# Feature-map attention and a cosine feed-forward on one core: the second products of a kept value in two steps, under a new order table

## The chip, the cores and the metric

One core of a Trainium2 chip runs the program. The metric is device time in microseconds (us). The engines are named as in the profile: PE (TensorE), DVE (VectorE), ACT (ScalarE), POOL (GpSimd) and SP (SyncE, which issues the DMAs here); PEld is PE's weight load.

## The reference

```python
def phi(x):                                    # x: batch 8, heads 8, 576 positions, 64
    proj = np.einsum('bhsd,df->bhsf', x, w_phi)             # 128 features
    proj = proj - np.max(np.abs(proj), axis=-1, keepdims=True)
    return np.concatenate([np.exp(proj), np.exp(-proj)], axis=-1)
q_p, k_p = phi(q), phi(k)
kv = np.einsum('bhsf,bhsd->bhfd', k_p, v);  z = np.sum(k_p, axis=2)
num = np.einsum('bhsf,bhfd->bhsd', q_p, kv)
den = np.einsum('bhsf,bhf->bhs', q_p, z)[..., None] + 1e-06
x = (num / den) as 4608 tokens x 512
h = x @ w_in                                   # 512 x 2048
out = (h * np.cos(h)) @ w_out                  # 2048 x 512, float32
```

## The kernel before

**The work.** Attention runs in 32 units of two heads each. A unit loads its q and k (`qk`, L530), projects q (L548, L551) and k (L594, L619), takes maxima, exponentiates on ACT, multiplies k's features with v (L698, L704) and q's features with that (L733, L739), divides on DVE, turns the result and stores it to DRAM (L770, L774). The first units have two `qk` tiles to take turns in; from the 22nd on all use one.

The feed-forward works on columns of 512 tokens. A float32 product is made of three matmuls: each operand is split into a high part (ACT, helper line L50) and a low part (DVE, helper line L55), and high·high, high·low and low·high are added up in a PSUM bank. Three columns go through `visit` (nine visits, L860 the first product, L907 to L909 the second). Six columns go in three pairs through `visit_two`, which makes the products of 2 x 2 blocks with seven multiplications instead of eight. Its first half (`products`, L1090) makes h; `wave` makes h·cos(h) with ACT and DVE (L1196, L1199, L1202, L1209) and keeps the values in tiles that other work has left. Its second half, `sweep`, goes over the kept values seven times: it combines some of them (DVE, L1257), splits each into `gh` (ACT) and `gl` (DVE) and multiplies them with slices of w_out that SP loads from DRAM (L1247) into the rings `wo_h` and `wo_l`, two tiles each.

**The second product before.** For one kept value, `mm2` in `sweep` (L1293) issues six matmuls as one step, three into each of two banks: `gh` with the slice's high part, `gh` with its low part, `gl` with its high part. The step depends on DVE's low step. `mm2` in `visit` does the same with four banks, two of them in a step (L907 gh, L908 gh, L909 gl). `gh` and `gl` are rings of three tiles.

**What sets the order.** All of this is written as `Step` objects with an engine and dependencies. `ORDER`, a table of step numbers written out by hand, says in which order the steps are issued; each engine executes its own steps in that order and waits in order. The costs in `Step` and its flag `port` (an operation of DVE or POOL that works on SBUF alone) enter no instruction; `plan` takes the order from the table and PSUM banks from who is last free. ACT loads another function table (`ACT_TABLE_LOAD`, L1435) wherever the order goes from a step with the sine to one with the exponential or back. Nothing but the order of issue and the semaphores of real dependencies keeps DVE and POOL apart.

Of the kernel before, what the change touches and what calls it, by code (L numbers as in the profile page):

```python
# [17 lines left out]
P = 128  # L18
# [8 lines left out]
def phi_attention_then_cos_ffn(ctx: ExitStack, tc: tile.TileContext, qkT, vS, w_phi, w_in, w_out, out, outT):  # L27
# [42 lines left out]
    class Step:  # L70
        def __init__(self, eng, cost, fn, deps=(), take=(), use=(), lat=None, table=None, port=False, kind="", pipe=0.0):
# [10 lines left out]
            for b in self.take + self.use:  # L82
# [5 lines left out]
    SHAPE = dict(mm1="full", mm2="full", one="full", wide="full", k_mm="upper", k_end="full", q_end="full", k_sub="full", kv_mm="left", x_mm="left", q_mm="upper")  # L88
    ORDER = [0, 3, 5, 4, 7, 8, 6, 9, 42, 58, 10, 11, 1, 44, 59, 46, 18, 60, 1265, 45, 64, 23, 61, 65, 66, 12, 48, 62, 17, 63, 19, 21, 13, 1266, 47, 24, 20, 68, 22,
# [701 lines left out]
    held = {}  # L791
# [3 lines left out]
    def visit(v):  # L795
# [46 lines left out]

        acc = [Buf("bank") for _ in range(NB3)]
        done = {}
        before = None
        for i, pr in enumerate(pairs):
            first, last = i == 0, i == len(pairs) - 1
            m = {}
# [29 lines left out]
            for r in range(2):  # L878
# [42 lines left out]
                for tbs in [[tb] for tb in range(NB3)] if fine else [[0, 1], [2, 3]]:  # L921
# [3 lines left out]
                    for tb in tbs:  # L925
                        done[tb] = before
                if first:
                    begun = before
# [573 lines left out]
```

## Time and profile before

| | |
|---|---|
| median of 3 runs | 993.64 us (993.25 to 995.34) |
| the profiled execution | 992.14 us |
| its span, first to last instruction | 990.4 us |
| PE, DVE, ACT, POOL busy | 99%, 86%, 80%, 21% of the span |
| granted TensorE clock | full in all slices |
| bytes moved | 211.67 MB, 214 GB/s |

Busy time of PE is the union of its matmuls' records. A record of a matmul with 512 columns lasts about 0.39 us, but the next one starts 0.23 us after it. So a delay of up to 0.16 us leaves no idle time in the profile, and whether PE waited is read from the starts of successive rows rather than from its busy share.

### The profile page before, as it was taken

Reading aid. Unit: us, or ns where it says so; the run is one execution under the profiler, and the core shown is the slowest. Engines: PE = TensorE matmul, PEld = TensorE weight load, DVE = VectorE, ACT = ScalarE, POOL = GpSimd, SP = SyncE. Lnnn points to the kernel's source line nnn. Section 1 sums busy time; section 2 is a strip of 40 time slices with the busy share of each in tenths; the row PEclk is TensorE's granted clock in tenths of the full one; section 3 lists DMA queues with packets and bytes.
Section 4 is the critical chain, followed back from the end, with each engine's and each line's share of the span. In section 5 each row is a group of like instructions: output and inputs, shape, how many; then the busy total and the mean of one; then the engine's idle time right before and its main releaser. Section 6 shows DMA issues by size and latency. Waiting matters only on the chain.

```text
span 990.4 us, 22351 instructions
## 1 busy us (share of the span) xinstructions
PE 982.9 (99%) x8586; PEld 796.7 (80%) x8586; DVE 855.3 (86%) x1494; ACT 790.3 (80%) x1560; POOL 203.5 (21%) x295
## 2 busy tenths in 40 slices
PE   9999999999999999999999999999999999999998
PEld 6778888888888888888778877788888888888886
DVE  7999999998899987878889679999886899776977
ACT  6899999878678868979998879788767776766663
POOL 4664442323232122201123210221000100000000
PEclk9999999999999999999999999999999999999999
DMA  7676865947587583777664746776566485664665
GB/s 255 207 218 194 258 211 172 344 136 232 191 278 243 187 289 126 235 251 273 217 208 164 231 140 205 229 256 214 177 204 215 152 266 182 241 226 160 181 191 191
DMA packets 118746, 211.67 MB, mean 214 GB/s; under 512 B 18672, under 2 KB 61808, under 8 KB 118640
## 3 DMA queue, kind: packets, MB, share of 16 engines
q1 hardware_dynamic: 118496, 210.18, 64.9%
q8 instruction: 67, 1.10, 0.5%
q14 instruction: 39, 0.32, 0.1%
q10 hardware_dynamic: 144, 0.07, 0.0%
HBM read 149.39 MB, written 60.82 MB: 212 GB/s over the span
## 4 chain that ended last, share of the span: by engine, by line
PE 81%; DVE 9%; ACT 5%; DMA 2%; issue 1%; POOL 1%; SPq 0%; DVEq 0%; POOLq 0%; ACTq 0%
PE bank L1090 21%; PE bank L1293 20%; PE bank L860 12%; PE bank L907 4%; PE bank L909 4%; PE bank L908 4%; PE bank L698 4%; PE bank L733 4%; PE bank L594 2%; PE bank L548 2%; ACT ek L652 1%; DVE gl L55 1%; DVE mk L632 1%; DVE m L565 1%; ACT eq L658 1%
## 5 line engine op out<-in xcount | busy, mean ns | idle before, releaser
L587 POOL TENSOR_TENSOR pq<-pq,bq 128x288 f32<-128x288 f32 x128 | 122.1, 982 | 112.0 <-DVE bq L583 110.5
L652 ACT ACTIVATE ek<-bank,mk 128x128 f32<-128x128 f32 x464 | 128.5, 409 | 6.7 <-DVE mk L635 5.9
L1293 PE MATMUL bank<-gh,wo_l 128*128 128x512 f32 x336 | 104.8, 393 | 0.2
L1293 PE MATMUL bank<-gh,wo_h 128*128 128x512 f32 x336 | 104.9, 394 | 0.0
L579 POOL COPY m<-m 32x36 f32<-32x36 f32 x96 | 29.9, 312 | 331.7 <-DVE m L574 308.0
L658 ACT ACTIVATE eq<-pq 128x576 f32<-128x576 f32 x128 | 81.2, 713 | 4.4 <-POOL pq L587 3.3
L1202 ACT ACTIVATE g<-g,halfpi 128x512 f32<-128x512 f32 x96 | 67.6, 718 | 19.4 <-DVE g L1199 19.0
L1435 ACT ACT_TABLE_LOAD x64 | 82.1, 1283 | 1.1
L1090 PE MATMUL bank<-xh_t,wi 128*128 128x512 f32 x192 | 75.8, 395 | 0.0
L733 PEld LDWEIGHTS bank<-kv,eq 128*64 128x64 f32 x2048 | 63.8, 138 | 13.1 <-issue 3.6
L1293 PEld LDWEIGHTS bank<-gh,wo_l 128*128 128x128 f32 x336 | 62.2, 188 | 14.7 <-ACT gh L50 1.1
L1293 PEld LDWEIGHTS bank<-gh,wo_h 128*128 128x128 f32 x336 | 62.2, 188 | 13.8 <-issue 0.5
L733 PE MATMUL bank<-kv,eq 128*64 128x65 f32 x2048 | 69.7, 223 | 0.0
L698 PEld LDWEIGHTS bank<-vs,ek 128*64 128x64 f32 x2048 | 62.5, 138 | 8.9 <-ACT ek L652 2.4
L1293 PE MATMUL bank<-gl,wo_l 128*128 128x512 f32 x168 | 66.1, 393 | 0.6 <-DVE gl L55 0.6
L698 PE MATMUL bank<-vs,ek 128*64 128x65 f32 x2048 | 66.4, 223 | 0.3 <-DVE g_qk L1209 0.2
L1199 DVE SCALAR_TENSOR_TENSOR g<-g,hs 128x512 f32<-128x512 int32 x72 | 51.5, 722 | 17.5 <-ACT g L1196 17.1
L1293 PE MATMUL bank<-gl,wo_h 128*128 128x512 f32 x168 | 65.6, 390 | 0.0
L632 DVE TENSOR_REDUCE mk<-bank 128x4 f32<-128x512 f32 (+1 forms) x96 | 50.6, 542 | 8.3 <-PE bank L594 8.2
L907 PE MATMUL bank<-wo_h,gh 128*128 128x512 f32 x144 | 57.7, 401 | 0.0
L1090 PE MATMUL bank<-xh_b,wi 128*128 128x512 f32 x144 | 57.4, 398 | 0.0
L565 DVE TRANSPOSE_TENSOR_REDUCE m<-pq 128x18 f32<-128x576 f32 x64 | 47.8, 759 | 9.9 <-ACT pq L561 8.6
(186 smaller groups left out, 2648.3 us busy)
## 6 DMA issues: line engine op xcount, KB each, us to landing
wi<-wi_parts SPq DMA_DIRECT2D x18, 1792.0 KB, 7.7
qk<-qkT SPq DMA_DIRECT2D x31, 640.0 KB, 5.1
wo_h<-wo_sums SPq DMA_DIRECT2D x24, 512.0 KB, 4.1
wo_l<-wo_sums SPq DMA_DIRECT2D x24, 512.0 KB, 3.9
x_raw<-xs SPq DMA_DIRECT2D x47, 256.0 KB, 3.9
wi_parts<-wi SPq DMA_DIRECT2D x12, 896.0 KB, 6.1
vs<-vS SPq DMA_DIRECT2D x32, 325.0 KB, 5.2
wo_l<-wo_parts SPq DMA_DIRECT2D x18, 512.0 KB, 5.3
```

The costliest lines, as they stand in the source:

```text
L587: qeng.tensor_tensor(out=d["pq"][:, c], in0=d["pq"][:, c], in1=d["bq"][:, c], op=ALU.subtract)
L632: DVE.tensor_reduce(out=m, in_=pv, axis=AX.X, op=ALU.max, apply_absolute_value=True)
L652: ACT.activation(out=e[:, g, s * P:(s + 1) * P], in_=pk[:, g, :], func=AF.Exp, scale=1.0 - 2.0 * s, bias=d["lk" if s == 0 else "mk", i][:, ...
L658: ACT.activation(out=e[:, s, :], in_=d["pq"][:, j * S:(j + 1) * S], func=AF.Exp, scale=1.0 - 2.0 * s)
L698: PE.matmul(out=acc[c:c + 64, n, i, :], lhsT=e[:, s, P * n + c:P * n + c + 64], rhs=vs[b["v"].slot][:, 2 * s + i, :], start=(s == 0 and i ...
L733: PE.matmul(out=ps[64 * h:64 * h + 64, 65 * g:65 * g + 65], lhsT=d["eq", j][:, n, c:c + 64], rhs=d["kv"][:, 2 * n + j, :], start=h not in ...
L860: PE.matmul(out=bank(b), lhsT=w[:, part, 2 * r + kt // 2, kt % 2 * P:(kt % 2 + 1) * P], rhs=d.get(("from", kt), d)[x, kt], start=(k == 0), ...
L907: PE.matmul(out=a, lhsT=gh[:, t], rhs=w[:, 0, r], start=first, stop=False)
L1090: PE.matmul(out=bank(bank_b), lhsT=w[:, part, block, j * P:(j + 1) * P], rhs=d[x, name, j], start=start and k == 0, stop=k == 5, skip_grou ...
L1202: ACT.activation(out=n["g"], in_=n["g"], func=AF.Sin, bias=halfpi, scale=1.0)
L1293: PE.matmul(out=bank(out[j]), lhsT=w[:, place, part, j * P:(j + 1) * P], rhs=n[x], start=start and i == mine[0] and q == 0, stop=i == mine ...
L1435: ACT.preload_act_table(AF.Exp if held == "e" else AF.Sin)
```

## The change

In both second products the step that needs `gh` alone is set apart. `mm2` now issues the matmuls with `gh` (four for two banks) and depends on ACT's high step; a new step `mm2l` issues those with `gl` (two) and depends on DVE's low step and on `mm2`. In `visit` the result of a bank is read out when that bank's own `mm2l` is done. At the end of the program, where the last kept value had two steps of three matmuls, it has one of four and two of one (`onel`). `ORDER` is a new table for all engines. A variable is renamed.

```diff
-    ORDER = [0, 3, 5, 4, 7, 8, 6, 9, 42, 58, 10, 11, 1, 44, 59, 46, 18, 60, 1265, 45, 64, 23, 61, 65, 66, 12, 48, 62, 17, 63, 19, 21, 13, 1266, 47, 24, 20, 68, 22,
...
+             4080, 4085, 4050, 4051, 4090, 4092, 4093, 4094, 4095, 4096, 4097, 4098, 4099, 4100, 4101, 4102]
...
-                def mm2(tbs, r=r, n=n, wo=wo, first=first, last=last):
+                def mm2(tbs, r=r, n=n, wo=wo, first=first):
                     w = w_tiles[wo]
...
-                        PE.matmul(out=a, lhsT=gl[:, t], rhs=w[:, 0, r], start=False, stop=last)
+                        PE.matmul(out=bank(acc[tb]), lhsT=n["gh"][:, t], rhs=w[:, 0, r], start=first, stop=False, skip_group_check=True)
+                        PE.matmul(out=bank(acc[tb]), lhsT=n["gh"][:, t], rhs=w[:, 1, r], start=False, stop=False, skip_group_check=True)
+
+                def mm2l(tbs, r=r, n=n, wo=wo, last=last):
...
-                    before = Step("PE", 0.68 * len(tbs), lambda tbs=tbs, mm2=mm2: mm2(tbs), [s7, before] + w_ready[wo],
+                    before = Step("PE", 0.455 * len(tbs), lambda tbs=tbs, mm2=mm2: mm2(tbs), [s6, before] + w_ready[wo],
...
+                for tbs in ([0, 1], [2, 3]):
+                    before_l = Step("PE", 0.2275 * len(tbs), lambda tbs=tbs, mm2l=mm2l: mm2l(tbs), [s7, before_l] + [hs_of[tb] for tb in tbs],
...
-            cp = Step(eng, 0.5 if eng == "ACT" else 0.61, out_copy, [before] + old, take=[] if old else [o],
+            cp = Step(eng, 0.5 if eng == "ACT" else 0.61, out_copy, [done[tb]] + old, take=[] if old else [o],
...
                 def mm2(js, n=n, box=box, place=place, i=i):
                     w = box["w"]
                     for j in js:
-                        for q, (part, x) in enumerate(((0, "gh"), (1, "gh"), (0, "gl"))):
-                            PE.matmul(out=bank(out[j]), lhsT=w[:, place, part, j * P:(j + 1) * P], rhs=n[x],
-                                      start=start and i == mine[0] and q == 0, stop=i == mine[-1] and q == 2, skip_group_check=True)
+                        for part in range(2):
+                            PE.matmul(out=bank(out[j]), lhsT=w[:, place, part, j * P:(j + 1) * P], rhs=n["gh"],
+                                      start=start and i == mine[0] and part == 0, stop=False, skip_group_check=True)
+
+                def mm2l(js, n=n, box=box, place=place, i=i):
+                    w = box["w"]
+                    for j in js:
+                        PE.matmul(out=bank(out[j]), lhsT=w[:, place, 0, j * P:(j + 1) * P], rhs=n["gl"],
+                                  start=False, stop=i == mine[-1], skip_group_check=True)
...
+                before = Step("PE", 0.91, lambda mm2=mm2: mm2((0, 1)), [h, ld, before] + (free.pop(id(out), []) if i == mine[0] else []),
+                              take=out if start and i == mine[0] else [], use=[gh, b] + ([] if start and i == mine[0] else out), kind=stage + "mm2")
                 for js in ((0,), (1,)) if end else ((0, 1),):
-                    before = Step("PE", 0.68 * len(js), lambda js=js, mm2=mm2: mm2(js), [lo, ld, before] + (free.pop(id(out), []) if i == mine[0] else []),
...
+                    before_l = Step("PE", 0.2275 * len(js), lambda js=js, mm2l=mm2l: mm2l(js), [lo, before, before_l], use=[gl, b] + out,
+                                    kind=stage + ("onel" if end else "mm2l"))
```

The table and the longer functions shift the line numbers: L594, L619, L548 and L551 of before are L605, L630, L559 and L562 of the change; L1293 is L1313 (gh) and L1319 (gl); L698 and L704 are L709 and L715, L733 and L739 are L744 and L750, L640 is L651, L530 is L541, L1247 is L1267, L774 is L785, L1320 is L1347, L1435 is L1462.

Place 1, PE, the start of the first sweep of the first pair. Before:

```order
L1293 MATMUL bank_69<-gh,wo_h 128x512 x2
L1293 MATMUL bank_69<-gl,wo_h 128x512
L1293 MATMUL bank_71<-gh,wo_h 128x512 x2
L1293 MATMUL bank_71<-gl,wo_h 128x512
L1090 MATMUL bank_73<-xh_b_5383,wi 128x512
L1090 MATMUL bank_73<-x_t_5699,wi 128x512
```

The change, from the second kept value on:

```order
L1313 MATMUL bank_71<-gh,wo_h 128x512 x2
L1313 MATMUL bank_75<-gh,wo_h 128x512 x2
L1319 MATMUL bank_71<-gl,wo_h 128x512
L1319 MATMUL bank_75<-gl,wo_h 128x512
L630 MATMUL bank_69<-wphi,qk 128x128
L1313 MATMUL bank_71<-gh,wo_l 128x512 x2
L1313 MATMUL bank_75<-gh,wo_l 128x512 x2
L744 MATMUL bank_76<-kv,eq 64x65 x16
L750 MATMUL bank_76<-kv,eq 64x65 x4
L744 MATMUL bank_74<-kv,eq 64x65 x16
```

Before, the one matmul with `gl` stands right behind the two with `gh` of its bank. Now the `gl` rows shown belong to the first kept value: the four matmuls with the second value's `gh` stand ahead of them, and the second's and the third's `gl` come behind the last row shown.

Place 2, PE, between the last read of one unit's `qk` tile and the first read of the next unit's, where both use the one tile (the 30th and the 31st unit). Before, with nine more rows of three kept values at the line of dots:

```order
L619 MATMUL bank_76<-wphi,qk 128x128
L1293 MATMUL bank_70<-gh,wo_h 128x512 x2
L1293 MATMUL bank_70<-gl,wo_h 128x512
L1293 MATMUL bank_69<-gh,wo_h 128x512 x2
...
L733 MATMUL bank_74<-kv,eq 64x65 x16
L733 MATMUL bank_71<-kv,eq 64x65 x16
L739 MATMUL bank_71<-kv,eq 64x65 x4
L698 MATMUL bank_76<-vs_89,ek 64x65 x32
L704 MATMUL bank_76<-vs_89,ek 64x130 x4
L594 MATMUL bank_73<-wphi,qk 128x128
```

The change, from the last row of eight that read the earlier unit's tile:

```order
L605 MATMUL bank_76<-wphi,qk 128x128
L709 MATMUL bank_75<-vs_88,ek 64x65 x32
L715 MATMUL bank_75<-vs_88,ek 64x130 x4
L1313 MATMUL bank_73<-gh,wo_h 128x512 x2
L1313 MATMUL bank_74<-gh,wo_h 128x512 x2
L1319 MATMUL bank_69<-gl,wo_l 128x512
L1319 MATMUL bank_71<-gl,wo_l 128x512
L630 MATMUL bank_70<-wphi,qk 128x128
```

The rows of `gh` stand there twice, for two kept values (eight matmuls in all). Before, 18 matmuls of kept values and three attention products stand between the two reads; now ten matmuls and one attention product.

Place 3, PE, the same thing at the start of the program, the fifth unit's load into the third's tile. Before:

```order
L619 MATMUL bank_74<-wphi,qk 128x128
L733 MATMUL bank_76<-kv,eq 64x65 x16
L739 MATMUL bank_76<-kv,eq 64x65 x4
L733 MATMUL bank_69<-kv,eq 64x65 x16
L619 MATMUL bank_70<-wphi,qk 128x128
L640 MATMUL bank_71<-mk,minus 128x512
L551 MATMUL bank_73<-qk,wphi 128x128
L640 MATMUL bank_75<-mk,minus 128x512
L548 MATMUL bank_72<-qk,wphi 128x512
L548 MATMUL bank_69<-qk,wphi 128x512
L594 MATMUL bank_71<-wphi,qk 128x128
```

The change:

```order
L559 MATMUL bank_72<-qk,wphi 128x512
L744 MATMUL bank_73<-kv,eq 64x65 x16
L744 MATMUL bank_69<-kv,eq 64x65 x16
L750 MATMUL bank_69<-kv,eq 64x65 x4
L651 MATMUL bank_74<-mk,minus 128x512
L709 MATMUL bank_75<-vs_89,ek 64x65 x16
L715 MATMUL bank_75<-vs_89,ek 64x130 x4
L630 MATMUL bank_76<-wphi,qk 128x128
```

Before, the third unit's tile is read last in the first row and the fifth unit's first in the last row, with nine rows between. Now six rows stand between.

Counted over the whole order: PE goes from one shape of matmul to another (full 128 x 128, 128 rows by half the columns, or half the rows) 161 times before and 154 times in the change; ACT loads a function table at L1435 64 times before and 48 times in the change.

## Rows read from the trace of the kernel before

**Rows 1.** The page's first part: busy us, share of the span and count of instructions of each engine.
```profile
PE 982.9 (99%) x8586; PEld 796.7 (80%) x8586; DVE 855.3 (86%) x1494; ACT 790.3 (80%) x1560; POOL 203.5 (21%) x295
```

**Rows 2.** The waits view of PE, whole: who waited for whom, us in total, times, longest.
```profile
PE bank L1430 <- DVE warm L292: 1.1, 1, 1.1
PE bank L594 <- DMA qk<-qkT: 0.7, 1, 0.7
PE bank L1293 <- DVE gl L55: 0.6, 2, 0.4
PE bank L594 <- ACT ek L649: 0.2, 1, 0.2
PE bank L640 <- DVE mk L632: 0.2, 1, 0.2
PE bank L619 <- DMA xs_tail<-xt: 0.2, 1, 0.2
PE bank L698 <- DVE g_qk L1209: 0.2, 1, 0.2
```

**Rows 3.** The timeline of all engines at the first sweep: start, us, engine, line, operation, tiles, count, and in brackets an idle time and what ended it.
```profile
486.89 2.79 POOL L587 TENSOR_TENSOR pq<-pq,bq 128x288 f32<-128x288 f32 x3
...
487.77 1.24 DVE L1199 SCALAR_TENSOR_TENSOR g<-g,hs 128x512 f32<-128x512 int32 x1 [1.80 <-ACT g L1196]
...
488.93 1.29 DVE L1257 TENSOR_TENSOR g_wo_xl<-g_wo_xl,g_wi_x 128x512 f32<-128x512 f32 x1
...
490.07 0.61 PE L1293 MATMUL bank<-gh,wo_l 128*128 128x512 f32 x2
...
490.95 0.68 DVE L1209 TENSOR_TENSOR g_wi_x<-hs,g 128x512 f32<-128x512 f32 x1
491.08 0.50 PE L1293 MATMUL bank<-gl,wo_l 128*128 128x512 f32 x1 [0.39 <-DVE gl L55]
...
491.88 0.40 PE L1293 MATMUL bank<-gl,wo_l 128*128 128x512 f32 x1
...
492.41 0.73 PE L1293 MATMUL bank<-gh,wo_l 128*128 128x512 f32 x2
...
493.14 0.50 PE L1293 MATMUL bank<-gl,wo_l 128*128 128x512 f32 x1
```

**Rows 4.** PE's timeline a little later, in the same sweep and the next one.
```profile
504.44 0.40 PE L1293 MATMUL bank<-gl,wo_l 128*128 128x512 f32 x1
504.77 1.15 PE L733 MATMUL bank<-kv,eq 128*64 128x65 f32 x32
...
509.92 0.61 PE L1293 MATMUL bank<-gh,wo_l 128*128 128x512 f32 x2
510.55 0.50 PE L1293 MATMUL bank<-gl,wo_l 128*128 128x512 f32 x1
...
511.73 0.71 PE L1293 MATMUL bank<-gh,wo_l 128*128 128x512 f32 x2
512.67 0.50 PE L1293 MATMUL bank<-gl,wo_l 128*128 128x512 f32 x1 [0.23 <-DVE gl L55]
```

**Rows 5.** PE's timeline in the sweeps of the second pair.
```profile
791.85 0.39 PE L1293 MATMUL bank<-gl,wo_l 128*128 128x512 f32 x1
...
792.34 0.73 PE L1293 MATMUL bank<-gh,wo_l 128*128 128x512 f32 x2
...
793.07 0.50 PE L1293 MATMUL bank<-gl,wo_l 128*128 128x512 f32 x1
```

**Rows 6.** ACT's table loads at L1435, a group of the page: count, busy us, mean ns of one, idle time before them.
```profile
L1435 ACT ACT_TABLE_LOAD x64 | 82.1, 1283 | 1.1
```

**Rows 7.** PE's timeline between 17 and 29 us, at the start of the program. An attention matmul is in float32 and has two records: x64 is 32 matmuls.
```profile
17.92 2.09 PE L698 MATMUL bank<-vs,ek 128*64 128x65 f32 x64
19.84 0.61 PE L704 MATMUL bank<-vs,ek 128*64 128x130 f32 x8
20.38 1.13 PE L548 MATMUL bank<-qk,wphi 64*128 64x512 f32 x4
...
22.08 1.15 PE L733 MATMUL bank<-kv,eq 128*64 128x65 f32 x32
...
24.33 0.49 PE L619 MATMUL bank<-wphi,qk 128*128 128x128 f32 x2
24.66 1.02 PE L640 MATMUL bank<-mk,minus 128*128 128x512 f32 x2
25.52 0.38 PE L551 MATMUL bank<-qk,wphi 128*128 128x128 f32 x2
...
28.05 1.16 PE L594 MATMUL bank<-wphi,qk 64*128 64x128 f32 x16 [0.23 <-ACT ek L649]
```

**Rows 8.** The page's DMA issues, the loads of `qk`: count, KB each, median us from issue to landing.
```profile
qk<-qkT SPq DMA_DIRECT2D x31, 640.0 KB, 5.1
```

**Rows 9.** The timeline around the 30th unit's `qk`: SP's issue of the load and PE's first read of the tile.
```profile
632.24 2.07 SPq L530 DMA_DIRECT2D qk<-qkT  x1
...
639.82 1.16 PE L594 MATMUL bank<-wphi,qk 64*128 64x128 f32 x16 [0.65 <-DMA qk<-qkT]
```

**Rows 10.** The end of the program: ACT's copies out of the last two banks.
```profile
985.92 0.39 ACT L1402 ACTIVATE o<-bank 128x256 f32<-128x256 f32 x1 [2.94 <-PE bank L1293]
...
986.60 0.38 ACT L1402 ACTIVATE o<-bank 128x256 f32<-128x256 f32 x1 [0.29 <-PE bank L1293]
```

More of the change, by code (lines that the diff above doesn't have):

```diff
@@ L844, in visit @@
         done = {}
-        before = None
+        before = before_l = None
         for i, pr in enumerate(pairs):
@@ L899, in low @@
                     lo_of(DVE, n["gl"], n["g"], n["gh"])
-                def mm2(tbs, r=r, n=n, wo=wo, first=first, last=last):
+                def mm2(tbs, r=r, n=n, wo=wo, first=first):
                     w = w_tiles[wo]
-                    gh, gl = n["gh"], n["gl"]
                     for tb in tbs:
                         t = slice(tb * P, (tb + 1) * P)
-                        a = bank(acc[tb])
-                        PE.matmul(out=a, lhsT=gh[:, t], rhs=w[:, 0, r], start=first, stop=False)
-                        PE.matmul(out=a, lhsT=gh[:, t], rhs=w[:, 1, r], start=False, stop=False)
-                        PE.matmul(out=a, lhsT=gl[:, t], rhs=w[:, 0, r], start=False, stop=last)
+                        PE.matmul(out=bank(acc[tb]), lhsT=n["gh"][:, t], rhs=w[:, 0, r], start=first, stop=False, skip_group_check=True)
+                        PE.matmul(out=bank(acc[tb]), lhsT=n["gh"][:, t], rhs=w[:, 1, r], start=False, stop=False, skip_group_check=True)
+                def mm2l(tbs, r=r, n=n, wo=wo, last=last):
+                    w = w_tiles[wo]
+                    for tb in tbs:
+                        t = slice(tb * P, (tb + 1) * P)
+                        PE.matmul(out=bank(acc[tb]), lhsT=n["gl"][:, t], rhs=w[:, 0, r], start=False, stop=last, skip_group_check=True)
                 g, gh, gl = (Buf(k) for k in ("g", "gh", "gl"))
@@ L920, in visit @@
                 fine = first
+                hs_of = {}
                 for tbs in [[tb] for tb in range(NB3)] if fine else [[0, 1], [2, 3]]:
-                    before = Step("PE", 0.68 * len(tbs), lambda tbs=tbs, mm2=mm2: mm2(tbs), [s7, before] + w_ready[wo],
+                    before = Step("PE", 0.455 * len(tbs), lambda tbs=tbs, mm2=mm2: mm2(tbs), [s6, before] + w_ready[wo],
                                   take=[acc[tb] for tb in tbs] if first else [],
-                                  use=[gh, gl] + w_slot[wo] + ([] if first else [acc[tb] for tb in tbs]), kind=stage + ("one" if fine else "mm2"))
+                                  use=[gh] + w_slot[wo] + ([] if first else [acc[tb] for tb in tbs]), kind=stage + ("one" if fine else "mm2"))
                     for tb in tbs:
-                        done[tb] = before
+                        hs_of[tb] = before
+                for tbs in ([0, 1], [2, 3]):
+                    before_l = Step("PE", 0.2275 * len(tbs), lambda tbs=tbs, mm2l=mm2l: mm2l(tbs), [s7, before_l] + [hs_of[tb] for tb in tbs],
+                                    use=[gl] + w_slot[wo] + [acc[tb] for tb in tbs], kind=stage + "mm2l")
+                    for tb in tbs:
+                        done[tb] = before_l
                 if first:
-                    begun = before
+                    begun = before_l
         for tb in range(NB3):
@@ L1250, in fetch @@
             slices[k, two] = (b, box, Step("SP", 0.38, load, need, take=[b], kind=stage + "fold_load", pipe=1.45))
-        before = None
+        before = before_l = None
         readers = {(i,) + k: [] for i in range(NP) for k in kinds}
@@ L1267, in sweep @@
         def sweep(at_half, k, key, out, start, form=None):
-            nonlocal before
+            nonlocal before, before_l
             mine = range(at_half * np_, (at_half + 1) * np_)
@@ L1299, in sweep @@
                 end = final and k == "a10" and i == NP - 1
+                before = Step("PE", 0.91, lambda mm2=mm2: mm2((0, 1)), [h, ld, before] + (free.pop(id(out), []) if i == mine[0] else []),
+                              take=out if start and i == mine[0] else [], use=[gh, b] + ([] if start and i == mine[0] else out), kind=stage + "mm2")
                 for js in ((0,), (1,)) if end else ((0, 1),):
-                    before = Step("PE", 0.68 * len(js), lambda js=js, mm2=mm2: mm2(js), [lo, ld, before] + (free.pop(id(out), []) if i == mine[0] else []),
-                                  take=out if start and i == mine[0] else [], use=[gh, gl, b] + ([] if start and i == mine[0] else out),
-                                  kind=stage + ("one" if end else "mm2"))
-                    ends[js] = before
-            return before
+                    before_l = Step("PE", 0.2275 * len(js), lambda js=js, mm2l=mm2l: mm2l(js), [lo, before, before_l], use=[gl, b] + out,
+                                    kind=stage + ("onel" if end else "mm2l"))
+                    ends[js] = before_l
+            return before_l
         free, ends = {}, {}
@@ L1430, in phi_attention_then_cos_ffn @@
             PE.matmul(out=banks[7][:, 0:P], lhsT=warm, rhs=warm, start=True, stop=True, skip_group_check=True)
-        held = None
+        held_set = None
         for x in plan():
-            if x.eng == "ACT" and x.table not in (None, held):
-                held = x.table
-                ACT.preload_act_table(AF.Exp if held == "e" else AF.Sin)
+            if x.eng == "ACT" and x.table not in (None, held_set):
+                held_set = x.table
+                ACT.preload_act_table(AF.Exp if held_set == "e" else AF.Sin)
             x.fn()
```

3 lines of the change are left out of this document (2 added, 1 removed), and 302 rows, old and new, of the table ORDER.

## The prediction

> **What bounds the kernel now.** I read the share of each engine first, then PE's waits, then PE's timeline where it waits. PE is busy in 982.9 of 990.4 us and no other engine is above 86% [rows 1]. So nothing is gained by making another engine faster; what can be gained is the time in which PE stands, and what can be lost is new standing. The waits view puts that at 3.2 us in seven entries, of which 1.1 us is the start of the program [rows 2]. The view shows too little: a matmul of 512 columns is followed by the next after 0.23 us while its record lasts 0.39 us, so the first 0.16 us of a delay are hidden. The starts give the delay. In the sweep, the two `gh` matmuls of a bank take 0.46 us from start to start; the `gl` matmul behind them comes after 1.01 us at 491.08 and after 0.73 us at 493.14 [rows 3], after 0.63 us at 510.55 and 0.94 us at 512.67 [rows 4], and after 0.73 us at 793.07 [rows 5]. It is late by 0.55, 0.27, 0.17, 0.48 and 0.27 us, 1.7 us together, and where an idle time is left its end is DVE's `gl`. Two `gh` matmuls are late as well, by 0.30 us (491.88 to 492.41, less 0.23) [rows 3] and 0.26 us (791.85 to 792.34) [rows 5]; those depend on ACT's high step.
>
> **The split (removes 1.7 us).** It adds no matmul and removes none: six per kept value before, four and two now. It takes DVE's low step from the dependencies of the first four. At the first sweep the second value's `gh` matmuls now stand ahead of the first value's `gl` (place 1), so at least four matmuls, 0.9 us, lie between a value's `gh` and its `gl`. That is more than the longest of the five delays, 0.55 us. I take all 1.7 us as gone. If the order leaves `gl` right behind elsewhere, the gain is nearer to none; zero is the other bound. The finer steps themselves I cost at nothing: the same matmuls stand in the same queue, and a wait that really holds one is counted in the terms below.
>
> **The order's shapes (remove 0.7 us).** PE changes the shape of its matmuls 154 times for 161. From a full matmul to one of half the columns the pitch is 0.33 us (504.44 to 504.77) for 0.23 us [rows 4]. Seven times 0.10 us is 0.7 us; other pairs of shapes may cost half of it, so 0.35 us is the lower bound.
>
> **The other late steps (remove 1.2 us).** These are the two late `gh` (0.30 and 0.26 us), the wait at 28.05 us for ACT (0.2 us [rows 2]) and three waits of 0.2 us [rows 2], 1.4 us together. ACT loads its function table 48 times for 64; 16 times 1283 ns [rows 6] is 20.5 us of ACT, on no path in itself, since ACT stands idle for a fifth of the span [rows 1]. But one load is longer than any of these delays, and each stood behind ACT's queue or DVE's. I take 1.2 us. The new order deals every such step anew, so the bounds are 1.4 us gained and 1.4 us lost.
>
> **The loads of `qk` (add 1.0 us).** Here the new order moves PE's reads closer to a transfer. With one tile, SP may issue a unit's load when PE has read the last unit's tile for the last time, and PE's next read waits for the landing; the whole of PE's queue waits behind it, and so in turn do ACT and DVE. At place 2 the rows between are now one product with v, 2.46 us (17.92 to 20.38) [rows 7], and ten matmuls of 0.23 us: 4.8 us. The load takes 5.1 us in the median [rows 8], so PE is 0.3 us late at least; the load of the unit before took 7.6 us (632.24 to 639.82) [rows 9], which would make it 2.8 us. I take 1.2 us, nearer to the median of 31 loads than to the one. At place 3 there stand two products with q's features, 2.25 us (22.08 to 24.33), one L640, 0.86 us (24.66 to 25.52), and half a product with v, 0.96 and 0.54 us [rows 7]: 4.6 us, 0.5 us short. Before, more stood between in both places. Against this the wait of 0.7 us for the 30th unit's load [rows 2, 9] goes, as its first read now stands further behind. 1.2 + 0.5 - 0.7 = 1.0 us. The slices of w_out are freed later, by the last `gl`, but at the shortest place in the order 23 matmuls stand between freeing and first use (5.2 us), no fewer than before (4.9 us); I cost that at nothing, and the cover is those matmuls.
>
> **The end (adds 0.2 us).** The last two banks were finished 0.68 us apart (three matmuls), and ACT copied each as it came [rows 10]. Now they end one matmul apart, 0.23 us, so the first copy starts 0.45 us later, and the second, behind it for 0.39 us on ACT, about 0.2 us later.
>
> **The sum.** -1.7 - 0.7 - 1.2 + 1.0 + 0.2 = -2.4 us, from 992.14 us of the profiled execution to 989.7 us. The median of the runs is 1.5 us above that execution; from 993.64 us it makes **991.2 us**.
>
> **What turns between DVE and POOL can give.** While POOL runs three L587 in 2.79 us, DVE's L1199 takes 1.24 us and its L1257 takes 1.29 us; L1209 with POOL idle takes 0.68 us [rows 3]. That is 1.2 us of DVE in one place, and the late `gl` at 491.08 follows it. The table can move POOL's work beside DVE's work in PSUM, but no semaphore holds the two apart, and each is held only by its place in its own queue. The Trainium skill ("SBUF — State Buffer", section "Who interferes with whom") says that a VectorE instruction with two inputs in SBUF and a GpSimd instruction that reads SBUF shut each other out for a whole instruction, and that whichever issues first goes first. The rows agree. By that rule the chip takes the turns already, and a table could only say who stands; that is the second rival.
>
> **Rivals.**
> *Nearly all waits go.* Both loads land in time (0 for 1.7 us), the 1.4 us go in full and half as much again of delays too short to be seen. -1.7 - 0.7 - 0.7 - 2.1 + 0.2 = -5.0 us: 988.6 us. For it: 20.5 us less on ACT. Against: place 2 has 4.8 us for a load that has a median of 5.1 us.
> *The turns give nothing.* DVE owes the port the same time as before, stands in other places, and its late low step keeps `gh` (three tiles) from being free, so ACT's high step and with it `mm2` come late instead of `gl`. Half of the 1.7 us stays, and the 1.2 us are dealt out again in full. -0.85 - 0.7 + 1.0 + 0.2 = -0.35 us: 993.3 us. For it: DVE is at 86% and in the sweeps does a combination and a low step for each kept value. Against: a value's `gl` has 0.9 us more.
> *The loads land late (slower).* Both new places see a landing like that at 632 us: 7.6 - 4.8 and 7.6 - 4.6 us, 5.8 us. With no gain from ACT: 5.8 - 0.7 - 1.7 - 0.7 + 0.2 = +2.9 us: 996.5 us. It decides from the landing time: two landings of 6.1 us eat the gain, two of 7.1 us make it slower by 2 us. For it: SP issues in order, and at place 2 four stores of `xs`, which wait for DVE, and a slice of w_out stand right ahead of the load. Against: the median of 5.1 us.
> That the change does not do what it says is ruled out for the split (place 1); for the turns it is the second rival.
>
> **How the numbers follow.** A measurement of this kernel tells about 0.2%, 2 us, from no change. The forecast has a chance of 0.36, the first rival 0.13 (both faster by more than that, though the forecast only just), the second 0.31 (the same), the third 0.20 (slower). The range goes from somewhat below the first rival, as its small delays are only bounded, to short of the third: 987.5 to 996.0 us.
>
> **What would show it.** Right: no wait of L1319 for `gl` at a sweep's start; the number of table loads at 48; PE waits for `qk` of some 0.5 and 1 us near 25 and 645 us; no wait for the 30th unit's load. Wrong: waits of PE for `gh` from ACT of 0.5 us and more in the sweeps (second rival); one wait for `qk` above 2 us (third); or waits in places that none of this names, as the table moved everything.

## The result and the profile after

The change makes the kernel slower by 1.1%: 1004.08 us median (1000.83 to 1008.98) against 993.44 us (992.49 to 995.34), a ratio of 1.0109 (1.0064 to 1.0153). Run again (label change_again) it took 1002.35 us against 992.62, 1.0105 (1.0089 to 1.0121). The forecast was 991.2 us, the range ended at 996.0. The profiled execution took 1000.83 us, its span is 999.1 us, 8.7 us more than before. One execution of a kernel below, that with the order of before up to 235 us, took 3443 us; nothing on record says why, and its ratio is without it.

The page's first part, which answers to [rows 1]:

```profile
PE 985.1 (99%) x8586; PEld 795.6 (80%) x8586; DVE 855.3 (86%) x1494; ACT 769.0 (77%) x1544; POOL 203.3 (20%) x295
```

DVE and POOL are busy for the same time as before, to 0.2 us: the new turns took nothing off them. ACT has 21.3 us less, nearly all of it table loads, now 48 for 64 [rows 6]:

```profile
L1462 ACT ACT_TABLE_LOAD x48 | 61.6, 1283 | 0.8
```

PE's waits, as in [rows 2]:

```profile
PE bank L630 <- DMA qk<-qkT: 1.4, 2, 1.1
PE bank L1313 <- DMA wo_h<-wo_sums: 1.3, 1, 1.3
...
PE bank L744 <- DVE o L959: 1.1, 1, 1.1
PE bank L923 <- DVE gl L55: 1.0, 1, 1.0
PE bank L709 <- ACT pq L570: 0.9, 1, 0.9
PE bank L605 <- DVE g L902: 0.7, 1, 0.7
...
PE bank L1313 <- ACT gh L50: 0.4, 1, 0.4
...
PE bank L1319 <- DVE gl L55: 0.2, 1, 0.2
```

In all 9.6 us for 3.2 before. To see the hidden part too I set every start of PE against the usual pitch of its kind. Starts over 0.125 us late sum to 12.9 us in 23 places, before to 5.7 us in 19. Sorted by what the chain behind each begins with, the change's are: 6.9 us a load that had not landed, 4.1 us a bank or input that ACT or DVE had not finished with, 1.4 us `gh` or `gl`, 0.5 us the program's start. Before, loads made 0.7 us and `gh` and `gl` 2.0 us. So 6.2 us of the 8.7 lie behind loads, and I look at these first.

Two are PE's own, at the places that the prediction named. PE's timeline at 25 and 653 us:

```profile
24.06 0.61 PE L715 MATMUL bank<-vs,ek 128*64 128x130 f32 x8
24.98 0.46 PE L630 MATMUL bank<-wphi,qk 128*128 128x128 f32 x2 [0.30 <-DMA qk<-qkT]
...
651.30 0.61 PE L1319 MATMUL bank<-gl,wo_l 128*128 128x512 f32 x2
652.99 0.46 PE L630 MATMUL bank<-wphi,qk 128*128 128x128 f32 x2 [1.08 <-DMA qk<-qkT]
```

The loads of `qk` land about as before [rows 8]:

```profile
qk<-qkT SPq DMA_DIRECT2D x31, 640.0 KB, 4.9
```

At 653 us the two `gl` matmuls fill PE until 651.75, so it is 1.24 us late; at 25 us it is 0.37 us. The third is a slice of w_out. SP's queue and PE at 945 us:

```profile
932.89 5.80 SPq L1267 DMA_DIRECT2D wo_l<-wo_sums  x2
938.78 0.42 SPq L1267 DMA_DIRECT2D wo_h<-wo_sums  x1
939.25 0.46 SPq L1347 DMA_DIRECT2D outT<-o  x1
941.05 0.36 SPq L1267 DMA_DIRECT2D wo_h<-wo_sums  x1
...
945.03 1.15 PE L1313 MATMUL bank<-gh,wo_h 128*128 128x512 f32 x4 [1.29 <-DMA wo_h<-wo_sums]
```

The second load of the first row went out at 938.33: SP stood 5 us for its tile to be emptied. That is slice 67. Slice 66, which PE needs two products sooner and whose tile was free, stands behind it in SP's queue. Issued 0.45 us behind it, 66 takes 6.1 us (the DMA issues of 938.7 to 939 us):

```profile
wo_h<-wo_sums SPq DMA_DIRECT2D x1, 512.0 KB, 6.1
```

It lands at 944.90; PE starts 0.13 us later, 1.46 us late. In the same stretch of the split alone (below) five such loads have a median of 3.7 us.

The rest comes through DVE and ACT, which issue in order and hold up all behind them. DVE's waits for DMAs in the change (before it had one, of 1.1 us, and none for `o`):

```profile
DVE o L959 <- DMA o<-sums: 8.8, 6, 2.2
DVE xt L770 <- DMA xs_tail<-xt: 1.2, 2, 0.7
```

L959 adds a fetched partial sum and so empties the bank that PE's next attention product takes (340 us). From issue to use a fetch has 7.3 us in the median, before 9.4; 6 of 24 are used within 0.3 us of landing, before one.

### The profile page after: what moved, and what is told of

Read it like the earlier page. It is cut to its first block, busy times and chain, and to the rows that moved or that the text cites. A ratio compares the mean times of both kernels' runs of the same rounds, so it can differ in the third digit from the quotient of the medians.

```text
span 999.1 us, 22265 instructions
## 1 busy us (share of the span) xinstructions
PE 985.1 (99%) x8586; PEld 795.6 (80%) x8586; DVE 855.3 (86%) x1494; ACT 769.0 (77%) x1544; POOL 203.3 (20%) x295
## 4 chain that ended last, share of the span: by engine, by line
PE 58%; DVE 19%; ACT 11%; DMA 7%; issue 3%; SPq 1%; POOL 1%; DVEq 0%; ACTq 0%; POOLq 0%
PE bank L1110 21%; PE bank L1313 12%; PE bank L1319 6%; PE bank L871 5%; PE bank L744 3%; DVE gl L55 3%; PE bank L709 3%; ACT ek L663 3%; PE bank L605 2%; PE bank L559 2%; DVE bq L594 2%; ACT eq L669 2%; DMA o<-sums 1%; DMA sums<-o 1%; DVE g L895 1%
## 5 line engine op out<-in xcount | busy, mean ns | idle before, releaser
L598 POOL TENSOR_TENSOR pq<-pq,bq 128x288 f32<-128x288 f32 x128 | 118.5, 954 | 77.9 <-DVE bq L594 59.5
L590 POOL COPY m<-m 32x36 f32<-32x36 f32 x96 | 34.5, 359 | 361.5 <-DVE m L585 357.7
L1313 PE MATMUL bank<-gh,wo_l 128*128 128x512 f32 x336 | 89.3, 394 | 0.4 <-ACT gh L50 0.4
L1313 PE MATMUL bank<-gh,wo_h 128*128 128x512 f32 x336 | 87.4, 394 | 1.3 <-DMA wo_h<-wo_sums 1.3
L744 PEld LDWEIGHTS bank<-kv,eq 128*64 128x64 f32 x2048 | 64.1, 138 | 14.5 <-issue 6.9
L1313 PEld LDWEIGHTS bank<-gh,wo_h 128*128 128x128 f32 x336 | 62.1, 188 | 16.0 <-ACT gh L50 1.9
L1313 PEld LDWEIGHTS bank<-gh,wo_l 128*128 128x128 f32 x336 | 61.9, 188 | 15.4 <-ACT gh L50 2.1
L744 PE MATMUL bank<-kv,eq 128*64 128x65 f32 x2048 | 70.0, 223 | 1.1 <-DVE o L959 1.1
L709 PEld LDWEIGHTS bank<-vs,ek 128*64 128x64 f32 x2048 | 62.7, 138 | 8.3 <-ACT ek L663 1.9
L709 PE MATMUL bank<-vs,ek 128*64 128x65 f32 x2048 | 66.8, 223 | 0.9 <-ACT pq L570 0.9
L1219 DVE SCALAR_TENSOR_TENSOR g<-g,hs 128x512 f32<-128x512 int32 x72 | 51.6, 722 | 13.8 <-ACT g L1216 13.3
L1120 ACT ACTIVATE hs<-bank 128x512 f32<-128x512 f32 x72 | 42.2, 597 | 23.2 <-PE bank L1110 19.1
L1216 ACT ACTIVATE g<-hs 128x512 int32<-128x512 f32 x72 | 45.7, 637 | 17.7 <-DVE hs L1134 11.3
L1110 PE MATMUL bank<-x_wi,wi 128*128 128x512 f32 x144 | 56.2, 390 | 0.0
L917 PE MATMUL bank<-wo_l,gh 128*128 128x512 f32 x144 | 56.2, 390 | 0.0
```

The costliest lines, as they stand in the source:

```text
L598: qeng.tensor_tensor(out=d["pq"][:, c], in0=d["pq"][:, c], in1=d["bq"][:, c], op=ALU.subtract)
L709: PE.matmul(out=acc[c:c + 64, n, i, :], lhsT=e[:, s, P * n + c:P * n + c + 64], rhs=vs[b["v"].slot][:, 2 * s + i, :], start=(s == 0 and i ...
L744: PE.matmul(out=ps[64 * h:64 * h + 64, 65 * g:65 * g + 65], lhsT=d["eq", j][:, n, c:c + 64], rhs=d["kv"][:, 2 * n + j, :], start=h not in ...
L917: PE.matmul(out=bank(acc[tb]), lhsT=n["gh"][:, t], rhs=w[:, 1, r], start=False, stop=False, skip_group_check=True)
L1110: PE.matmul(out=bank(bank_b), lhsT=w[:, part, block, j * P:(j + 1) * P], rhs=d[x, name, j], start=start and k == 0, stop=k == 5, skip_grou ...
L1313: PE.matmul(out=bank(out[j]), lhsT=w[:, place, part, j * P:(j + 1) * P], rhs=n["gh"], start=start and i == mine[0] and part == 0, stop=Fal ...
```

## The experiments

Each was timed in five rounds beside the kernel before; ratios are to that kernel. The files differ in the length of the table, so lines stand up to six further down than in the change (L1318 is its L1313). Two theories: **A**, the new table places loads too near their first use, on SP's queue or the user's; **B**, the loss is in the new places of the steps on ACT and DVE. Beside them: the split itself costs.

**The split alone.** The order of before on all engines (steps renumbered); each product's `gl` part directly behind its `gh` part.

```diff
-  ..., 2355, 2336, 2351, 2363, ...
+  ..., 2454, 2432, 2448, 2449, 2463, ...
```

> The order of before on every engine, with the split alone: each product's two matmuls with gl are a step of their own and stand directly behind its four with gh. Theory one (the loss is in the new places of the steps on ACT, DVE and SP, and the split costs nothing): 0 to 2 us below before, 991.5 to 993.5 us; PE's late starts for gl at the sweeps' first values (1.7 us before) shrink by 0.4 to 1.2 us, since each gl stands two or three matmuls later. Theory two (the split itself costs, by more waits on PE): 3 us and more above before, 996 to 1004 us. Within 0.2% of before would say that the split is worth nothing here either way.

991.64 us, 0.9993 (0.9984 to 1.0001). The split costs nothing that shows; it gives 0.7 us, not 1.7, and the interval holds zero. PE's timeline shows why (L1318 and L1324 are `gh` and `gl`):

```profile
490.35 1.07 PE L1318 MATMUL bank<-gh,wo_l 128*128 128x512 f32 x4
491.36 0.74 PE L1324 MATMUL bank<-gl,wo_l 128*128 128x512 f32 x2
492.69 1.19 PE L1318 MATMUL bank<-gh,wo_l 128*128 128x512 f32 x4 [0.59 <-ACT gh L50]
```

The `gl` that came 0.55 us late at 491.08 [rows 3] now comes 0.1 us late, and the next `gh` 0.76 us where it was 0.30: the wait moved to ACT's high step. The loss is in the order.

**The new order without the split.** On PE each `gl` part moved up behind its `gh` part.

```diff
- gh(1), gh(2), gl(1), gl(2)
+ gh(1), gl(1), gh(2), gl(2)
```

> The new order on every engine, with the split undone in the order: each product's two matmuls with gl stand directly behind its four with gh, wherever the new order had put them (by up to 11 steps of PE later). Theory one (the new places of the other engines' steps): as slow as the change or slower, 1003 to 1010 us, since gl is made for its later place. Theory two (the split costs): 994 to 999 us.

1037.21 us, 1.0453: PE's waits for `gl` come to 27.3 us. The new table needs the split.

**SP's queue as before.** SP's steps in before's order, the others in the change's.

```diff
- SP: order of the change
+ SP: order of before
```

> The change, with SP's queue (all loads and stores) back in the order of before, and the other engines' queues as in the change but for a step here and there that has to pass its neighbour. If the loads' new places are most of the loss (the waits for qk 1.6 us, wo_h 1.5 us, the o tile 1.1 us, x_raw 1.2 us of late starts): 996 to 1000 us, and no wait for wo_h or qk above 0.7 us. If the loss is made by the places on ACT and DVE: 1002 us and more, with new waits of PE in the attention.

1230.36 us, with six waits of PE for `qk` of 40.6 us together and one of 13.3 us for a bank. Two tables' queues don't mix; this decides nothing between A and B.

**The change again**, no edit.

> The change once more, unaltered, for the spread of its runs and a second profile. If its waits are fixed by the order, PE's waits for qk near 25 and 653 us, for wo_h near 945 us and for gl near 443 us come back within 0.5 us of their size; if they hang on how a transfer lands in a run, two or more of them are gone or over twice as long and others have come. Time 1001 to 1009 us under both.

Both happen. The waits at 25, 443, 653 and 945 us come back (0.55, 0.81, 0.96, 1.68 us late; the change had 0.37, 1.18, 1.24, 1.46). That at 25 us now bears ACT's name, but the load of `qk` lands 0.14 us ahead of it. Those at 75 and 340 us shrink to 0.24 and nothing, and a new one stands at 163 us, 1.85 us:

```profile
162.10 0.63 ACT L50 ACTIVATE xh_t<-x_raw 128x512 fp32r<-128x512 f32 x1 [1.37 <-DMA x_raw<-xs]
162.63 0.58 ACT L963 ACTIVATE o<-bank 128x512 f32<-128x512 f32 x1
...
163.27 1.16 PE L605 MATMUL bank<-wphi,qk 64*128 64x128 f32 x14 [1.36 <-ACT o L963]
```

ACT stands for a load of x, the copy behind it empties a bank, PE waits for the bank. PE's clock falls after it (stretch, then the busy us of five engines, the granted clock, DMA):

```profile
165.00:167.00 2.00, 2.00 (x7) 1.52 (x6) 1.97 (x4) 1.61 (x7) 0.31 (x1) 0.50 0.89 181
```

0.50 is the lower of its two levels, 1.2 GHz; eight matmuls come 0.2 us late each, 1.6 us. Two of the later profiles of such kernels show the same. The length of the wait alone doesn't decide it: at 945 us PE stands 1.5 us in this execution, and the granted clock behind it, from 946 to 950 us, is 1.00.

**A third `o` tile.** The order of the change; the warm-up reads an `o` tile, for the room.

```diff
-    ... hs=4, g=3, gh=3, gl=3, o=2, w_raw=1, w_t=1)
+    ... hs=4, g=3, gh=3, gl=3, o=3, w_raw=1, w_t=1)
-    warm = const.tile([P, P], F32, name="warm")
+    warm = new("o", [P, DM], F32, "o")[:, 0:P]
```

> The change in the same order, with three o tiles in place of two (the warm-up matmuls read the head of one of them, which frees the room). In the profile of the change DVE stands 8.8 us in six waits for loads of o, and SP 24.5 us in 13 waits for the store that has to empty the tile first; before DVE stood for one load, 1.1 us in all, and none of them was of o. Theory A (the new order puts these loads too near their use, and PE's waits near 340, 443 and 461 us come from there): DVE's waits for o fall below 3 us, PE's late starts at those places go, 998.5 to 1001 us against 1002.4 of the change. Theory B (DVE's waits for o are hidden, and the loss is in the places on ACT and DVE alone): DVE's waits fall as well, but the time stays within 1 us of the change.

1000.89 us, 1.0078 (1.0063 to 1.0092). DVE's waits for `o`:

```profile
DVE o L959 <- DMA o<-sums: 1.7, 1, 1.7
```

A's time, 2.7 us less than the change by the ratios, 1.5 by the medians. Not its places: 443 and 461 us stay (0.77 and 0.49 us late), and 340 us is late in one profile of two without the tile.

> The control: the split in the order of before, with the third o tile. Theory A: the old order leaves its loads of o 9.7 us between issue and use in the median, so the tile gives nothing, 991 to 992.5 us, within 0.1% of the split alone (991.6). If a third tile helps in any order, it comes out 1 us or more below the split alone.

The same tile in the old order: 991.89 us, 0.9988 (0.9980 to 0.9997), within 0.5 us of the split alone. As far as these two show, the tile helps only where the order leaves no room.

**Where it is lost.** The split, with one order up to a step of PE and the other from there on.

```diff
- ORDER = new
+ ORDER = steps of before's first part, in one order; the rest in the other
```

> The split; the order of the change up to the step at which PE stands near 470 us, the order of before from there on (23 steps pass one neighbour at the seam). PE's late starts over 0.125 us with a wait sum to some 9 us before 470 us in the change and to 3 us before; that would make 997 to 1000 us. If the loss is in the sweeps: 992 to 994 us.

1028.37 us: where the orders meet, five waits of 2 to 5 us stand between 449 and 503 us. The splice spoiled it; it says nothing on the halves.

> The split; the order of before up to the step at which PE stands near 470 us, the order of the change from there on. From the late starts behind 470 us (5 us in the change, 2.4 us before): 993.5 to 996 us. If the two halves add up, this one and the other half exceed the split alone together by what the change does, 10 to 11 us; if the change's loss needs both halves, they exceed it by less than 6 us.

996.89 us, 1.0039 (1.0027 to 1.0051), 4.6 us above the split alone and 0.9 above the range. Some 1.4 us of it are late starts at the seam (470 to 477 us); the two largest others are the loads at 653 and 945 us (at 649 and 941 us here, 1.53 and 1.43 us).

> The kernel with the order of before up to 470 us and the order of the change from there on (996.9 us), with two steps put back: slice load 66 ahead of 67 on SP, and the last product with qk of the 30th unit behind five neighbours on PE (before it stood 40 steps further back still). PE's late starts there are 1.43 and 1.53 us. Theory A (the loads' places): both go and the time falls by 2.5 to 3 us, 993.9 to 994.4 us. Theory B (other engines' places; the waits come back): 995.5 to 997 us.

Those two steps put back:

```diff
-  ..., 2858, 1204, 2851, ..., 2861, 2864, ..., 3793, 3881, 3893, ..., 3880, 3905, ...
+  ..., 2858, 2851, ..., 2861, 1204, 2864, ..., 3793, 3893, ..., 3880, 3881, 3905, ...
```

994.47 us, 1.0011 (1.0002 to 1.0019), 2.8 us less by the ratios, and the starts said 2.96. A holds here, though the median ends 0.1 us above its range. PE's longest waits now (the first is the program's start):

```profile
PE bank L1462 <- DVE warm L308: 1.1, 1, 1.1
PE bank L1318 <- DVE hs L1374: 0.4, 1, 0.4
```

> The split; the order of before up to the step at which PE stands near 235 us, the order of the change from there on. If the change's loss before 470 us (5.5 us) sits in the attention's first part, where DVE and ACT are busy 94% and more of the time (before 235 us), this comes out at 997 to 998.5 us, near the kernel cut at 470 us (996.9). If it sits in the visits and loads of o between 235 and 470 us: 1000 to 1002 us.

999.42 us, 1.0059 (1.0046 to 1.0072): between the two answers. From 235 to 470 us the new order costs some 2.0 us.

> The split; the order of before up to the step at which PE stands near 140 us, the order of the change from there on. If the wait near 163 us (1.7 to 2.2 us, and 1.4 to 1.6 us at the lower clock behind it, in three of the change's profiles) makes most of the first part's loss: 2 us and more above the kernel cut at 235 us, 1001 to 1003 us. If the waits for qk and vs near 25 and 75 us make it: 999 to 1000.5 us.

1000.73 us, 1.0074 (1.0060 to 1.0087): 1.5 us go with the order from 140 to 235 us, and the remaining 3.1 us, to the change's 1.0105, with the order before 140 us. Each difference is uncertain by some 1.8 us. That isn't where PE loses them: it passes 150 us in the change's two profiles 0.1 and 1.1 us sooner than here, and the second falls back by 4.0 us at 163 us. No wait stands at 163 us here: it needs what comes before it.

**Single repairs of the change.**

```diff
-  ..., 3793, 3881, 3893, ..., 3880, 3905, ...
+  ..., 3793, 3893, ..., 3880, 3881, 3905, ...
```

> The change, with two neighbours of SP's queue exchanged: the slice load 66 (into wo_h) stands ahead of 67 (into wo_l) again, as before. In the change's two profiles 66 waits behind 67 for 67's tile to be emptied, is issued together with it, takes 6.1 and 6.4 us instead of 3.6 to 4.4, and PE starts 0.13 us after it lands, 1.46 and 1.68 us late at 945 us. Theory A (the loss is loads that come too near their first use): 66 is issued some 3 us sooner, the wait is gone with no other in its place, and the time is 1.5 us below the change, 1000.5 to 1001.5 us. Theory B (the loss sits in the places of ACT's and DVE's steps): the wait there stays at 1 us or more, for gh from ACT, as the trace names ACT's gh too, and the time stays at 1002 to 1003 us.

SP's queue with slice 66 ahead of 67:

```profile
938.43 0.36 SPq L1272 DMA_DIRECT2D wo_h<-wo_sums  x1
939.33 0.36 SPq L1272 DMA_DIRECT2D wo_l<-wo_sums  x1
```

It lands after 3.7 us instead of 6.1, and PE's late start at 945 us is gone; for this wait B is wrong. It goes out only some 1.4 us sooner against PE, not 3 (this execution runs 1.0 us behind the change's here). Set start against start with the change's two profiles, PE gains 1.4 and 1.6 us there and keeps them to the end. The time, 1002.12 us, 1.0099 (1.0082 to 1.0116), doesn't show 1.5 us: its executions spread over 5 us.

```diff
-  SP: slice loads 66, 67, 68, 69, 70, 71, 72, 73, 74, 75, 76, 77, 78, 79
+  SP: slice loads 67, 66, 68, 69, 71, 70, 72, 73, 75, 74, 76, 77, 79, 78
```

> The split in the order of before, with the one exchange of slice loads done four times: 67 ahead of 66, and so 70 and 71, 74 and 75, 78 and 79. Theory A: each makes two loads issue together, the second lands after 5 to 6.4 us instead of 3.7, and PE stands 0.8 to 1.5 us each time; 3 to 6 us above the split alone, 995 to 997.5 us, with four waits of PE for wo_h. Theory B (a slice has room enough, and the wait in the change came from ACT): within 1 us of the split alone, 991 to 992.6 us.

993.01 us, 1.0009 (1.0000 to 1.0017), 1.6 us above the split alone: two of the four exchanges made PE late, by 0.65 and 0.31 us; the second load of these pairs took 5.4 and 5.0 us. The sign is A's, the size a third to a half. In the change a store of outT goes out right behind the pair (939.25), here none does; whether that makes the difference wasn't tried.

```diff
-  ..., 579, 1695, 1856, 1696, 1677, 565, ...
+  ..., 579, 1856, 1677, 1695, 1696, 565, ...
```

> The change, with one step of ACT moved past three: the copy that empties a bank (the fifth copy of the visits, L963) stands ahead of the high step of x that waits for its load of x_raw, and of the two steps between. In one of the change's two profiles and in that with three o tiles PE comes 1.74 to 1.85 us late near 164 us, for that bank, and works the next eight matmuls at the lower clock, 0.2 us each; in the other it comes 0.23 us late. Theory A: both go; the median falls by 2 to 3.4 us, 999 to 1000.5 us, and the spread of the runs shrinks. Theory B: the wait moves to another bank or to x itself, 1001.5 to 1003 us.

1004.25 us, 1.0115 (1.0091 to 1.0140). The wait at 163 us and the low clock are gone from the profile, but PE is 0.88 us late at 161 us and 1.1 us at 353 to 359 us: no gain.

> The same with the copy that empties the bank moved past three steps of ACT, ahead of the high step that waits for its load. If that wait is worth what its profiles show, 2 to 3 us below the kernel without the move; if the delay only changes its place, within 1 us of it.

The same move where the runs spread less: 999.50 us, 1.0067 (1.0054 to 1.0080), 0.7 us less, inside the uncertainty. But the wait it is aimed at isn't in that kernel's profile.

**Ten steps moved and the third tile** (the expectation counts one too many). With the exchange on SP, the copy on ACT and the product with `qk` at 653 us as above:

```diff
-  PE:  k_end 0, k_sub 4, q_end 3, k_mm 3, q_mm 3
+  PE:  k_sub 4, q_end 3, k_mm 3, q_mm 3, k_end 0
-  PE:  kv_mm 9, kv_mm 10, x_mm 4, kv_mm 11, k_end 5, q_end 5
+  PE:  x_mm 4, k_end 5, q_end 5, kv_mm 9, kv_mm 10, kv_mm 11
-  DVE: m.times 42, m.reduce 43, m.times 43, m.out_copy 24, m.out_copy 25
+  DVE: m.times 42, m.out_copy 24, m.reduce 43, m.out_copy 25, m.times 43
-  DVE: p.x_low 11, m.out_copy 28, p.x_low 9, p.x_sum 5, m.low 47
+  DVE: m.low 47, p.x_low 11, m.out_copy 28, p.x_low 9, p.x_sum 5
```

> The change with eleven of its 4103 steps moved by 1 to 7 places in their queues, and three o tiles: the two above (1.5 and 2.3 us); on PE the last product with qk of units 5 and 30 and three products with v, each behind two to five neighbours, so that the loads of qk near 25 and 653 us and of vs near 75 us have 1 to 2 us more (0.4, 1.2 and 1.1 us); on DVE one low step near 443 us ahead of two that wait for x_raw (0.8 us), and two copies near 391 us into gaps ahead of the steps that leave them (0.8 us); the o tile (1.5 us). Theory A: the sum is 9.6 us less, 993 us; with new waits behind the old ones for a third of it, 996 us: 992 to 997 us. Theory B: less than half of the loss comes back, 998 us and more.

1000.76 us, 1.0077 (1.0063 to 1.0090): 2.8 us came back, not 5 to 10. The moved waits are gone and others stand beside them:

```profile
PE bank L567 <- DMA xs_tail<-xt: 1.4, 1, 1.4
PE bank L567 <- DMA qk<-qkT: 1.2, 1, 1.2
...
PE bank L1115 <- ACT bank L1133: 0.9, 1, 0.9
```

The product with `v` moved back at 75 us brought the next unit's read of `qk` forward: L567 is 1.63 us late at 78 us. Before 470 us A isn't shown as the whole cause, nor is any single step.

**Less work on POOL.**

```diff
+            c = slice(j * HALF, j * HALF + 16)
             qeng.tensor_tensor(out=d["pq"][:, c], ...
```

> The change with GpSimd's L598 on 16 of its 288 columns (the rest of the subtraction is left out, so the attention's numbers are others); its 118.5 us shrink by 80 to 100 us, the port is free for DVE, and the step's users get their input sooner. If the first half's loss is that DVE and ACT are full there and can't make good a wait for a load: PE's late starts between 25 and 470 us fall to a half or less, 996 to 999 us. If the loads' places alone make it (PE's own wait for qk and vs, ACT's for x_raw): within 1.5 us of the change, 1001 to 1003 us.

> The control: the split in the order of before with the same subtraction on 16 columns. It has about 1.5 us of late starts between 25 and 470 us, so under both theories 989.5 to 991.5 us.

997.76 us, 1.0051 (1.0039 to 1.0063), and 987.74 us, 0.9946 (0.9934 to 0.9958). The change gains 5.4 us, the control, for which I had expected 2 at most, 4.7: the distance between them stays 10 us. But they don't gain in the same places. The order of PE is the same with and without the edit, so the same matmul can be set against itself, here two of the change and then of the light kernel:

```profile
26.13 0.38 PE L562 MATMUL bank<-qk,wphi 128*128 128x128 f32 x2
473.64 1.16 PE L605 MATMUL bank<-wphi,qk 64*128 64x128 f32 x16
...
27.45 0.38 PE L562 MATMUL bank<-qk,wphi 128*128 128x128 f32 x2
470.97 1.16 PE L606 MATMUL bank<-wphi,qk 64*128 64x128 f32 x16
```

From 25 to 470 us the light kernel gains 4.0 us on this profile of the change and 5.0 us on the second; the control gains nothing there on the split alone (-0.1 us). Behind 470 us the change gains 0.9 and 0.3 us more, the control 3.7. So in the stretch that the first theory speaks of, its answer comes out: the time is in its range, and late starts between 25 and 470 us fall from some 6 and 7 us to 3.8. PE's own waits for `qk` and `vs` stay (0.7 us at 26 us, 0.8 at 75); those at 163, 340, 391 and 461 us, which come through ACT and DVE, are gone. The places of the loads alone don't make that loss. By which way POOL's subtraction has a part in it isn't shown: DVE is busy 841.2 us for 855.3, and ACT gets its input sooner as well.

More than half of what the control gains, all behind 470 us, is its waits for `gh` and `gl` (2.5 us of late starts in the split alone), none of which is left in PE's list:

```profile
PE bank L1463 <- DVE warm L308: 1.1, 1, 1.1
PE bank L1116 <- ACT bank L1134: 0.4, 1, 0.4
PE bank L611 <- DMA qk<-qkT: 0.3, 1, 0.3
PE bank L657 <- DVE mk L649: 0.2, 1, 0.2
PE bank L636 <- ACT ek L669: 0.2, 1, 0.2
```

Its DVE is busy 840.2 us for 854.6 of the split alone, with the same instructions: 14.4 us had gone to instructions that took longer beside POOL's. Nearly all of it (14.3 us by the sums of their times) is in those with two inputs in SBUF; those that read a bank take what they took. The Trainium skill ("SBUF — State Buffer", section "Who interferes with whom") has the two engines shut each other out there, and the number agrees. The new turns had that time to win and won none of it (DVE is busy 855.3 us before and in the change).

## Why the prediction was wrong

- **The step that failed** is "the other late steps": "The new order deals every such step anew, so the bounds are 1.4 us gained and 1.4 us lost." I bounded new delays by the old ones. An order made anew isn't bounded by what the last one left: loads alone make 6.9 us of late starts for 0.7, banks another 4.1. Without the loads of `qk`, the slice and `gh` or `gl`, the late starts of the change sum to 8.4 us, those of before to 3.0: 5.4 us lost where I took 1.2 as gained. Behind 470 us two loads' places are the cause, shown by putting them back (2.8 us). Before 470 us the new order costs 6.6 us or somewhat more, as the late starts at the seam aren't in the change. Loads stand behind most of the late starts there in each profile; repairs of their places returned only part, and less work on POOL returned 4 to 5 us with every load in its place. So the places of the loads alone don't make that loss; through which steps it comes stays open.
- **The slices of w_out at nothing**: wrong by 1.46 us. I measured the room from the tile's freeing, 5.2 us, and didn't ask what stands ahead of the load on SP, nor what else is in transfer.
- **The split**, -1.7 us: measured -0.7 (-1.6 to +0.1), so not even the sign is clear of noise. With `gl` out of the way the next `gh` is the wait. The five delays themselves are 1.45 us when each `gl` is set against the matmul right ahead of it: in three of them the two `gh` already stood 0.1 us further apart than usual.
- **The loads of `qk`**, +1.0 us: right. 0.37 and 1.24 us for 0.5 and 1.2, less the 0.7 of the 30th unit, is +0.9. They landed after 4.9 and 5.8 us. The 1.2 was a choice between 0.3 and 2.8, so that it fits so closely is partly luck.
- **The shapes**, -0.7 us: the usual pitches of all starts sum to 1.0 us less. **The end**, +0.2 us: ACT now copies both banks in one go, where before the first copy went 0.68 us ahead [rows 10], and from the last matmul's start to the end of the span it is 4.65 us for 4.22, +0.4. Late starts (+7.2), shapes and end make 6.6 of the 8.7 us; the rest lies in delays too short to be counted.

```profile
994.61 0.66 ACT L1429 ACTIVATE o<-bank 128x256 f32<-128x256 f32 x2 [2.03 <-PE bank L1319]
```

- **The rivals.** "The turns give nothing" was right on DVE and POOL, but not on the time. "The loads land late" had the sign and the mechanism with the wrong load: `qk` needed no landing of 7.6 us, since loads of `vs`, `wo_h`, `o` and x, which I had costed at nothing or not at all, took part in it. The range stopped at 996.0 us, short of this rival's 996.5, though it had a chance of 0.20; and 996.5 is still 6 to 8 us too low.
- **The signs.** Nearly all that were to show the forecast right came: 48 table loads, waits for `qk` of 0.37 and 1.24 us, none for the 30th unit's load, and little waiting for `gl` in the sweeps. So did the last of those against it, waits in places that nothing names. Signs at the places one has looked at say little about an order that moved everything.

Open: why the change's executions spread over 8 us where those of before spread over 3. The wait at 163 us, worth 3.4 us with the clock behind it, is there in some profiles and not in others, but taking it away didn't narrow the spread. With less work on POOL the change's five executions lie within 2.4 us; why isn't known.

The fastest kernels here that compute all of it are the split in the old order, without and with the third tile (991.6 and 991.9 us); with the tile it is 0.12% (0.03 to 0.20) faster than before.

## What to carry to other kernels

When an order is dealt anew, list every load with its room, from where SP can issue it (behind what stands ahead of it in the queue) to its first use, and set that against landings of loads that go out together; the waits of the old profile bound nothing. A wait taken from one producer shows the next one: price a split by the second-latest input. A profile of one execution can miss or overstate a wait behind a transfer, so take two before repairing it. And where an edit gains as much on a control, ask where each of them gains before calling a theory dead.

## What the hardware showed

Two loads of 512 KB issued 0.45 us apart landed after 4.4 and 6.1 us, where the same loads 2.7 us apart took 3.7. A wait of PE of 1.4 us at 163 us was followed by eight matmuls at 0.43 instead of 0.23 us, at the lower clock, while after 0.9 us at 74.5 us, and after 1.5 us at 945 us in the same execution as the first, the granted clock was 1.00. And a subtraction that keeps POOL busy for 12% of the span, cut from 288 to 16 columns, gave 4.7 us to a kernel whose PE is 99% busy, and 14.4 us to DVE with the same instructions.
